# A transformer block in a written-out order: the condition's load alone on ScalarE's queue, the first loads in one row on SyncE's, and a new order of all 786 operations

## The chip, the cores and the metric

The kernel runs on one core of one Trainium2 chip. Its engines work in parallel, each through its own list of instructions: TensorE (PE; its weight loads are shown as PEld), VectorE (DVE), ScalarE (ACT), GpSimd (POOL) and SyncE (SP), which here only issues transfers. ScalarE can issue transfers too. The metric is the device time of one execution in microseconds (us).

## What is computed

One block: an attention part A and a token-mixing MLP part B, both behind a layer norm whose scale and shift come from a condition vector c. S is 2048 rows, D 512 columns, all inputs bf16.

```python
mod = silu(c) @ w_mod                      # six rows of 512: sa, ca, ga, sb, cb, gb
h = layernorm(x) * (1 + ca) + sa
x = x + ga * A(h)       # qkv = h @ wqkv; 32 heads of 16; each row attends to
                        # itself and the rows 2, 4, ..., 14 before it; then @ wo
h = layernorm(x) * (1 + cb) + sb
x = x + gb * B(h)       # layer norm, then per column: gelu(h^T @ w1 + b1) @ w2 + b2, over
                        # the 2048 rows, with 1792 hidden units
```

## The kernel before

**Operations and their order.** The kernel first describes its work as 786 named operations (`G.add`, `G.add_any`, lines 51 to 84), each with what it reads and writes, and for many with several engines to choose from. The text ORDER (lines 191 to 249) then gives the order of all of them by hand. `schedule` (86 to 125) walks through it: a letter behind a colon picks the engine (`a` ScalarE, `d` VectorE, `p` GpSimd, `s` SyncE), `q` on a TensorE operation cuts each matmul into four with 32 weight columns each, `n` leaves a matmul out whose addition another engine then makes, `+` lets VectorE make that addition. `fill:n` puts idle matmuls on TensorE, n pieces of 128 columns each (`fill_fn`, 528 to 531: in matmuls of 512 as far as they go, the rest in single pieces); they multiply the identity and are never read. `schedule` also hands out the six PSUM banks, the four `big` buffers and the five `vd` buffers in that order. Each engine executes its operations in the order of the text and waits at each one until what it needs is there; so an operation that waits holds up all that stand behind it on its engine. All instructions are issued through one helper, so they all show line 142 in the profile, and tiles tell them apart.

**The start.** SyncE and ScalarE issue the first loads: x tiles 0 and 1 (`ld_x0`, `ld_x1`, 431), the four tiles of chunk 1 in two loads (`ld_x_1_2`, `ld_x_1_4`, 455 to 458), c (`ld_c`, 429), two parts of w_mod (`ld_wmod1`, `ld_wmod0`, 434 to 437), wqkv in three parts. `dma2` (381) is a load that either queue can issue. Eight transfers can be under way without a wait; the ninth waits until the first has landed, and so on. GpSimd makes the identity; `act_table` (518) loads ScalarE's function table. `cps` (535) turns c into columns on TensorE, `silu_exp` (ScalarE) and `silu_dve` (VectorE) make silu(c). `modcols1` (551) multiplies it by a part of w_mod and gives `a1col`, the scale of the first norm, by which the weights wqkv (`wsc`, 446 to 453) or, for the first two chunks, the transposed rows (`hT`, 676 to 680) are scaled. `modcols0` gives, by a copy `sab` on ScalarE, the shift, which `qvb` (559 to 568) turns into biases of q and v. The modulation rows for all else come later (`modrow`, `mrows`, 570 to 604), over a store and a load (`st_row`, `ld_row`).

**Attention in five chunks** of 2, 4, 4, 4 and 2 tiles of 128 rows (`build_chunk`, 616 to 913). For a tile: statistics on VectorE or ScalarE (`ln1s`, with a small VectorE step `ln1v`), `rstd1` on ScalarE, `nb1` on VectorE, the normalised row (`n1`). Then the transpose (`tr` on TensorE and `hT`, or a transposing transfer `xt`), the projections on TensorE (`qkv{chunk}_{0 q, 1 k, 2 v}{part}`) and their evictions from PSUM (`ev`). Per chunk VectorE multiplies q by the shifted k (`qk`, four large products), TensorE sums over the head (`red`), VectorE takes the maximum (`max`), TensorE subtracts it (`sub`), ScalarE takes the exponent (`exp`), TensorE adds up (`esum`), ScalarE inverts (`rcp`), VectorE scales (`smB`), four transfers move the weights to other partitions (`a2`), four others copy v (`vd`); VectorE multiplies them (`pv`, four large products), TensorE sums (`pvacc`), ScalarE evicts (`oev`), and `wo` projects a tile. `x1` adds the residual, `ln2`, `n2`, `aff`, `ln3` and `h3` are the next two norms.

**The MLP.** The first matmul of B runs over the rows, so it needs the norm of all tiles. It is cut in sweeps (`mlp1_0`, `mlp1_1`, `mlp1_2`) that run as tiles get ready; between sweeps partial sums are parked in SBUF (`park`, 978) and added back (`padd`) or put in by a matmul (`inj`). `gelu` follows on ScalarE, `mlp2` for 16 row tiles on TensorE, `fin` on VectorE, `st_out` stores. The last row tile is cut in three pieces (`mlp2_15_0` to `mlp2_15_2`, 1004).

Of the kernel before, what the change touches and what calls it, by code (L numbers as in the profile page):

```python
# [197 lines left out]
qvb_cp0:a ev0_00:a ln1s12:a ev0_02:d qkv1_13 ld_wqkv2 qkv0_20 ln1v13 qk0_3 qk0_2 ev1_13:a qk0_0 qvb1 ln1v12 qkv0_22:q  # L198
ld_wrow0 red0_0 ev1_00:a qkv1_03:q ev1_10:a qk0_1 red0_1 red0_2 red0_3 mask qvb_cp1:a ev0_20:a ev0_22:a wsc1_2:p
halo_v1:a qk1_0 ev1_03:a wsc1_3:a qkv1_11:q ld_wmod2 wsc2_3:a modrow0 ld_b1 mrows0:a ev1_11:a ld_wrow2 qkv1_02 max0  # L200
wsc0_2:p ld_wo0 n1_7:p sub0 rstd1_3 qkv1_01 ld_wo2 exp0 qkv1_12:q wsc1_1:p esum0:q qk1_3 red1_0 ev1_01:a qk1_1
ev1_02:a biascols n1_6:p ld_wrow1 rcp0 smB0 ev1_12:a ld_x_4_14 ln1s14:a qkv1_22 qk1_2 a2_0_2:a xt6 ld_wrow3 modrow1
red1_1 a2_0_1:a n1_9:p wsc2_0:d ln1s15:a ln1v14 nb1_3 n1_11:a qkv1_23:q mrows1 qkv1_21 ev1_21:a red1_2 red1_3 xt8
ev1_23:a fill:1 n1_10:p qkv1_20 ev1_20:a ev1_22:a qkv2_13 qkv2_10 wsc0_1:p vd0_2 ev2_13:a ln1v15 vd0_1 max1 sub1
qkv2_00 exp1 a2_0_0:s a2_0_3:s pv0_1 vd0_0 pv0_0 st_row0 pv0_2 qkv2_03 esum1:q ld_wo3 pvacc0_0 vd0_3 halo_v2:p
biascols_cp:a pvacc0_1 pv0_3 pvacc0_2 pvacc0_3 ev2_10:a ev2_00:a qk2_0 n1_13:a n1_12:a ld_row0 woq_s rcp1 smB1
oev0_2:a qkv2_11 qkv2_02:q ev2_03:a qk2_3 qkv2_01:q red2_0 oev0_0:a wo0:q wsc2_1:a wsc2_2:a qkv2_12 ev2_11:a ev2_01:a
ev2_02:a ev2_12:a wo1 qkv2_21:q a2_1_1:a qkv2_22 x1_1:a ln2q1:a x1_0:a xt10 ln2q0:a qk2_1 qkv2_23 xt12 qk2_2 a2_1_0:s
halo_k3:a ln2m0 vd1_2 a2_1_2:s qkv3_12 a2_1_3:s pv1_2 rstd1_4 red2_1 nb1_4 vd1_0 st_row1 red2_2 red2_3 rstd2_0
ev2_22:a nb2_0 ev2_21:a qkv3_13:q ev3_13:a max2 vd1_3 pv1_0 n1_14:a vd1_1 pvacc1_2 n1_15:a qkv2_20:q ev2_20:a sub2  # L210
qkv3_22:q ev3_12:a pv1_1 qkv3_10 exp2 ev2_23:a halo_v3:a qkv3_20 n2_0:a oev1_2:a ev3_10:a esum2 rcp2 qkv3_00 ev3_22:a
qkv3_02:q ev3_00:a pv1_3 ev3_02:a pvacc1_0 ev3_20:a qkv3_01:q ev3_01:a qkv3_11:q xt14 ld_row1 n2_1:p vd2_3 pvacc1_1
smB2 aff0 qk3_0 vd2_1 fill:1 vd2_0 oev1_0:a oev1_1:a pvacc1_3 ev3_11:a qk3_1 qkv3_23:q oev1_3:a a2_2_2:s ln3s1:a
qkv3_03:q wo4 a2_2_1:s qk3_2 a2_2_0:s ev3_03:a ev3_23:a x1_4:a ln2q4:a wo2 x1_2:a a2_2_3:s red3_0 wo3:q x1_3:a ln2q3:a
qkv3_21:q ev3_21:a wo5 red3_1 pv2_3 x1_5:a vd2_2 qk3_3 qkv4_20:q red3_2 qkv4_22 red3_3 qkv4_12 fill:18 ln2q5:a
ld_w1_0_512 ln2q2:a ln2m2 pv2_0 pvacc2_0 vd3_0 ev4_20:a ln3s0:a ln3v0 ev4_12:a rstd2_2 ev4_22:a ln3v1 qkv4_02 oev2_0:a
ln2m4 rstd2_4 nb2_2 n2_2:a max3 sub3:q exp3 pvacc2_3 oev2_3:a qkv4_10:q pv2_2 vd3_2 esum3 nb2_4 pv2_1 vd3_1 n2_3:p
ld_w1_0_0 n2_5:a rcp3 smB3 pvacc2_2 fill:14 a2_3_0:s a2_3_1:s a2_3_3:s n2_4:a qkv4_00:q oev2_2:a rstd3_0 aff2 pvacc2_1
oev2_1:a wo6 wo9 wo7 aff4 nb3_0 ln3s2:d ev4_02:a ln3s3:a ln3v3 h3_1:p wo8 a2_3_2:s ev4_00:a ln3v2 ld_w2_0 ln3s4:d
rstd3_2 nb3_2 x1_9:a ln3s5:a h3_0:p mlp1_0_6_0:q x1_7:a ln3v4 x1_8:a h3_3:d mlp1_0_1_0 h3_2:d mlp1_0_6_2 mlp1_0_1_2  # L220
pv3_1 mlp1_0_5_0:q ln3v5 ev4_10:a ld_w1_0_896 x1_6:a mlp1_0_3_0:q mlp1_0_3_2:q ln2q7:a pvacc3_1 rstd3_4 mlp1_0_5_2:q
# [854 lines left out]
```

## Time and profile before

| | us |
|---|---|
| median of 3 runs | 201.75 (201.44 to 202.0) |
| the profiled execution | 202.11 |
| its span, first to last instruction | 200.4 |
| TensorE, VectorE, ScalarE, GpSimd busy | 191.0, 159.6, 128.6, 18.6 |
| matmuls, weight loads, VectorE, ScalarE instructions | 1818, 1836, 241, 306 |

The profile shows one execution. Its times count from the first instruction, so 1.7 us of the execution's time lie around the span. The rows used below have a start, a duration, the engine, the operation, out<-in tiles with shapes, the count, and in brackets the idle time of the engine ahead of it with what ended it. An engine's name with a q (ACTq, SPq) is its issuing part. A weight load shows when TensorE takes up a matmul; a matmul's own end is modelled, and matmuls overlap, so pace is read from starts.

### The profile page before, as it was taken

What the parts mean: (1) busy time and instruction counts of PE and PEld (TensorE: products, weight loads), DVE (VectorE), ACT (ScalarE), POOL (GpSimd) and SP (SyncE); (2) the same over time, 40 slices, a digit from 0 to 9 for tenths busy, and PEclk for the clock granted to TensorE, in tenths of its full rate; (3) what the DMA queues carried; (4) which work ended last, traced back from release to release, by engine and by line L of the source; (5) the groups of instructions that cost most, each with busy time, mean ns of one, the idle gap of its engine ahead of it and who ended that gap; (6) DMA issues with size and microseconds to landing.
All of it is one profiled execution on the core that took longest, in us unless ns stands there. A gap on an engine that the chain in (4) does not pass through costs nothing.

```text
span 200.4 us, 4572 instructions
## 1 busy us (share of the span) xinstructions
PE 191.0 (95%) x1818; PEld 95.8 (48%) x1836; DVE 159.6 (80%) x241; ACT 128.6 (64%) x306; POOL 18.6 (9%) x45
## 2 busy tenths in 40 slices
...
GB/s 161 341 355 350 176 240 127 160 56 185 300 143 321 220 167 194 176 112 311 64 310 257 36 184 196 160 186 234 338 244 298 85 26 52 27 52 52 174 52 52
DMA packets 53889, 35.95 MB, mean 179 GB/s; under 512 B 24428, under 2 KB 50668, under 8 KB 53868
## 3 DMA queue, kind: packets, MB, share of 16 engines
...
q10 hardware_dynamic: 1640, 0.46, 1.0%
q8 instruction: 14, 0.23, 0.5%
...
## 4 chain that ended last, share of the span: by engine, by line
PE 69%; DVE 22%; issue 4%; DMA 1%; ACT 1%; ACTq 0%; DVEq 0%
PE psS L142 67%; DVE big L142 14%; PE psL L142 3%; DVE st L142 2%; DVE h L142 2%; DMA c_t<-in_c_dram 1%; DVE mv L142 1%; ACT h L142 1%; DVE lsb L142 1%; DVE m L142 1%; DVE nb L142 0%; ACTq L142 0%; DVE woq L142 0%; DVE hT L142 0%; ACT rb L142 0%
## 5 line engine op out<-in xcount | busy, mean ns | idle before, releaser
L142 PEld LDWEIGHTS <-wst 128*128 128x128 bf16 (+1 forms) x536 | 34.9, 101 | 33.7 <-issue 4.0
L142 PE MATMUL psS<-h,wst 128*128 128x512 bf16 (+1 forms) x333 | 50.3, 380 | 0.5 <-issue 0.3
L142 DVE TENSOR_TENSOR big<-q_sb,k_f 128x4096 bf16<-128x4096 bf16 (+1 forms) x20 | 36.6, 1859 | 0.4 <-ACT q_sb L142 0.4
L142 DVE TENSOR_TENSOR big<-a2sb,vD 128x4096 bf16<-128x4096 bf16 (+1 forms) x20 | 36.5, 1860 | 0.2
L142 PE MATMUL psS<-hT,w_qkv 128*32 128x512 bf16 (+3 forms) x360 | 29.7, 346 | 0.0
L142 DVE SCALAR_TENSOR_TENSOR h<-psS,bcol,rows_bc 128x512 f32<-128x512 f32 (+2 forms) x17 | 12.1, 710 | 22.1 <-PE psS L142 20.6
L142 PEld LDWEIGHTS <-w_qkv 128*32 128x32 bf16 (+1 forms) x402 | 19.4, 109 | 17.8 <-issue 4.4
L142 PE MATMUL psS<-gT,big 128*128 128x512 bf16 x110 | 24.7, 379 | 0.1
L142 PEld LDWEIGHTS <-big 128*128 128x128 bf16 x144 | 12.0, 97 | 13.5
L142 ACT ACTIVATE junk<-xx 128x512 bf16<-128x512 bf16 x26 | 16.3, 627 | 3.3 <-DVE xx L142 1.4
L142 PE MATMUL psS<-woq,o_sb 128*32 128x512 bf16 (+1 forms) x107 | 15.7, 380 | 0.9 <-ACT o_sb L142 0.6
L142 ACT ACTIVATE gT<-psS,bcol 128x512 bf16<-128x512 f32 x14 | 9.0, 685 | 8.1 <-DVE psS L142 8.0
L142 POOL TENSOR_SCALAR h<-xx,rs,nb 128x512 bf16<-128x512 bf16 x9 | 6.9, 766 | 75.6 <-DVE nb L142 36.5
L142 DVE TENSOR_TENSOR psS<-psS,gT 128x512 f32<-128x512 f32 x14 | 9.3, 695 | 5.0 <-PE psS L142 5.0
L142 ACT ACTIVATE h<-xx,nb,rs 128x512 bf16<-128x512 bf16 x16 | 12.4, 808 | 0.5 <-DVE nb L142 0.4
L142 PEld LDWEIGHTS <-ident 128*32 128x32 bf16 (+1 forms) x137 | 7.0, 102 | 10.5 <-issue 5.9
L142 PE MATMUL psS<-ident 128*128 128x512 bf16 (+1 forms) x35 | 10.6, 450 | 1.4 <-POOL epscol L142 1.4
L142 PE MATMUL psS<-hT,wst 128*32 128x512 bf16 (+2 forms) x110 | 11.7, 352 | 0.1
L142 DVE TENSOR_TENSOR h<-h,xx 128x512 bf16<-128x512 f32 (+2 forms) x17 | 11.1, 653 | 0.6
L142 DVE TENSOR_TENSOR h<-h,rows_bc 128x1024 bf16<-128x1024 bf16 (+2 forms) x16 | 10.9, 689 | 0.4
L142 DVE BATCH_NORM_STATS2 st<-xx 128x6 f32<-128x512 bf16 x12 | 7.9, 680 | 3.9 <-DMA xx<-in_A_x_dram 3.8
L142 ACT ACTIVATE v_sb<-psS,qvb 128x512 bf16<-128x512 f32 (+1 forms) x20 | 11.0, 595 | 0.0
...
## 6 DMA issues: line engine op xcount, KB each, us to landing
...
out_dram<-h SPq DMA_DIRECT2D x15, 128.0 KB, 1.8
...
```

The source lines that it names most:

```text
L142: r = fn(*a, **k)
```

## The change

- c can be loaded by either queue (`dma2`), and the order picks ScalarE's, behind the table load. `ld_x_1_2`, which stood ahead of c on that queue, goes to SyncE, so that SyncE issues ld_x1, ld_x0, ld_x_1_4, ld_x_1_2, ld_wmod1, ld_x_2_8, ld_wqkv0 and all that follows in one row.
- The idle matmuls of the start, 4 pieces ahead of `cps`, then 64 and 4 behind it, become 6 and 68 pieces behind it. The later ones, 13, 1, 1, 18 and 14 pieces, become 13, 7, 1 and 22; 26 and 6 pieces stand behind the last store of the text.
- `tr0_0` moves ahead of `modcols1`. The four qkv0 groups of q and k now stand ahead of `modcols0`, with the 7 idle pieces between `modcols0` and `qvb0`.
- All else is in a new order. 786 names in both; some 40 operations change their engine and some 45 TensorE operations change between whole matmuls and the cut form. `wo10` makes its residual on TensorE again and `x1_10` goes from VectorE to ScalarE. `rstd1_4` and `nb1_4` move up from chunk 2 to a place ahead of `pv0`; `gsc` moves from the first output tiles to the last ones.

```diff
 ORDER = """
-ident ld_x_1_2:a halo0 ld_c consts ld_x1:s ld_x0:s ld_x_1_4:s act_table ln1s3:d fill:4 cps ld_wmod1 silu_exp silu_dve
-fill:64 ln1s1:a ln1s2:a ln1s0:d ln1v1 ld_x_2_8 ln1v0 ln1s4:d ld_wqkv0 rstd1_0 nb1_0 n1_1:a fill:4 ln1v4 n1_0:p ln1s5:d
-ln1v2 ln1v5 ln1v3 rstd1_1 nb1_1 ld_x_2_6 modcols1 n1_2:d n1_5:d ln1s8:a a1col wsc0_3:p n1_4:d tr0_0 hT0_1:a hT0_3:a
-n1_3:d hT0_0:a fill:13 hT0_2:a ld_wqkv1 ld_wmod0 ln1s9:d ld_x_3_10 ln1s6:d tr1_0 tr1_2 hT1_2:a ln1v6 qkv0_02 ln1v9
-hT1_0:a qkv0_12 qkv0_10 ln1s7:d ln1v7 ln1v8 rstd1_2 hT1_3:d wsc1_0:a ev0_12:a modcols0 sab:a ld_x_3_12 nb1_2 n1_8:a
-qkv0_00 qvb0 wsc0_0:p ev0_10:a ld_b2 ld_wo1 hT1_1:d qkv1_00 ln1s11:d ln1s10:d ln1s13:d qkv1_10:q ln1v11 ln1v10
...
+ident act_table ld_c:a cps silu_exp silu_dve ld_x1:s ln1s1:d ln1v1 ld_x0:s ln1s0:a ld_x_1_4:s ld_x_1_2:s ln1v0
+ld_wmod1 ln1s3:d rstd1_0 ln1s5:d nb1_0 ln1v3 n1_0:p ln1s4:d ln1v5 ln1s2:a ln1v2 halo0 fill:6 n1_1:p fill:68 tr0_0
+ld_x_2_8 ln1v4 ld_wqkv0 consts rstd1_1 nb1_1 n1_5:a n1_2:d n1_3:d ln1s9:d modcols1 a1col ld_x_2_6 n1_4:a ln1s8:d
+wsc0_1:p ln1v8 hT0_3:a tr1_2 hT0_1:a ld_wqkv1 ld_wmod0 ld_x_3_10 wsc1_3:p hT0_2:a wsc0_2:d hT0_0:a tr1_0 ln1s6:d
+fill:13 hT1_1:a qkv0_02:q ld_x_3_12 qkv0_00 ld_wo3 hT1_0:d hT1_3:a qkv0_12 hT1_2:a wsc1_2:a ln1v9 ln1s7:d wsc0_0:p
+ln1v6 ln1v7 rstd1_2 ev0_12:a nb1_2 n1_6:a qkv0_10 ln1s10:d modcols0 sab:a wsc1_1:p ld_wqkv2 n1_7:a ln1s11:d fill:7
+qvb0 qvb_cp0:a ln1s13:d ev0_10:a ev0_00:a qkv1_03 qkv1_10 ln1s12:a ev1_10:a ln1v10 qkv1_00 ln1v13 ev0_02:d ev1_03:a
...
+a2_0_0:s rstd1_4 a2_0_3:s red1_2 red1_3 max1 qkv2_00:q n1_11:a qkv1_20 ev2_00:a nb1_4 st_row0 ev1_20:a
...
+fin10_0 st_out10_0 st_out8_0 fin11_0 st_out11_0 fin13_0 st_out13_0 mlp2_12_0 mlp2_14_0 fin12_0 mlp2_15_0 gsc fin14_0
+st_out12_0 st_out14_0 fin15_0 st_out15_0 mlp2_15_1 fin15_1 mlp2_15_2 st_out15_1 fin15_2 st_out15_2 fill:26 fill:6
 """
...
-    add("act", 0.55, lambda: nc.scalar.dma_start(c_t[:], c[0].rearrange("(t p) -> t p", p=P)), writes=["c_t"],
-        name="ld_c", lat=2.0)
+    dma2(c_t[:], c[0].rearrange("(t p) -> t p", p=P), D * 4, ["c_t"], "ld_c")
```

More of the change, by code (lines that the diff above doesn't have):

```diff
@@ L197 @@
-qkv0_00 qvb0 wsc0_0:p ev0_10:a ld_b2 ld_wo1 hT1_1:d qkv1_00 ln1s11:d ln1s10:d ln1s13:d qkv1_10:q ln1v11 ln1v10
[L198 to L221, printed above, removed]
@@ L227 @@
-mlp1_0_7_0 ld_w2_3 park0_4:a ln3v6 mlp1_0_7_2 park0_5:a ln3v9 x1_11:a ln2q12:a mlp1_0_8_0 mlp1_0_8_2 park0_6:a wo13:n
-ln3s7:a ln3v7 sub4 mlp1_0_10_0 mlp1_0_9_0 x1_13:d exp4 rstd3_6 nb3_6 esum4 mlp1_0_8_4 ln2q13:a ln2m12 mlp1_0_10_2
-mlp1_0_10_4 mlp1_0_9_2 rcp4 mlp1_0_7_4 h3_8:d rstd2_12 mlp1_0_12_0 mlp1_0_12_2 mlp1_0_12_4 smB4 a2_4_1:a a2_4_0:s
-mlp1_0_9_4 a2_4_2:s h3_9:d a2_4_3:a h3_7:d nb2_12 h3_6:p mlp1_0_7_6 ln2q11:a park0_7:a x1_10:d mlp1_0_8_6 ld_w1_0_1664
-ln2q10:a park0_8:a n2_13:p mlp1_0_9_6 park0_9:a n2_12:d aff12 ln2m10 rstd2_10 mlp1_0_10_6 park0_10:a ln3s13:a pv4_2
@@ new lines @@
+qkv1_13 qk0_1 red0_1 red0_2 red0_3 wsc0_3:p ev0_20:a qk1_0 ld_wo1 ld_wrow2 mask ev1_13:a qkv1_01:q n1_8:a ld_wo0 max0
+wsc2_3:a ld_wrow3 ld_wrow0 ln1s14:a qkv1_11:q ev1_11:a modrow1 xt6 qk1_3 ev1_01:a ld_wmod2 sub0:q exp0 qkv1_22
+ev1_22:a qkv1_02 qk1_1 esum0:q vd0_3 xt8 ln1v12 ev1_02:a vd0_0 rcp0 smB0 qkv1_12:q vd0_1 ev1_12:a qk1_2 wsc2_2:d
+rstd1_3 a2_0_1:a nb1_3 mrows1 modrow0 a2_0_2:a mrows0:a ln1v14 red1_0 red1_1 qkv1_23 halo_v1:p ln1s15:a ln1v15 qkv1_21
+ev1_21:a a2_0_0:s rstd1_4 a2_0_3:s red1_2 red1_3 max1 qkv2_00:q n1_11:a qkv1_20 ev2_00:a nb1_4 st_row0 ev1_20:a
```

65 lines of the change are left out of this document (43 added, 22 removed).

## The prediction

> **What bounds the kernel now.** I read the page first, then the windows by stage, then the chain of waits in order of time. On the page the line of busy times, and the shares of the chain by engine:
>
> ```profile
> PE 191.0 (95%) x1818; PEld 95.8 (48%) x1836; DVE 159.6 (80%) x241; ACT 128.6 (64%) x306; POOL 18.6 (9%) x45
> ...
> PE 69%; DVE 22%; issue 4%; DMA 1%; ACT 1%; ACTq 0%; DVEq 0%
> ```
>
> TensorE looks like the one bound, but the averages hide stages. Busy time by stage (stretch, its length, then PE, PEld, DVE, ACT, POOL, each with its count):
>
> ```profile
> 19.00:42.00 23.00, 22.72 (x388) 12.80 (x383) 22.60 (x23) 20.52 (x47) 2.00 (x3) 1.00 0.71 171
> 42.00:58.00 16.00, 15.43 (x184) 6.73 (x184) 15.76 (x14) 14.47 (x32) 0.77 (x1) 1.00 0.58 180
> 58.00:104.00 46.00, 44.77 (x625) 22.80 (x628) 45.63 (x50) 44.59 (x112) 2.46 (x4) 1.00 0.69 209
> 104.00:121.00 17.00, 16.76 (x113) 7.95 (x118) 16.55 (x35) 14.83 (x41) 1.53 (x2) 1.00 0.66 177
> ...
> 132.00:198.00 66.00, 65.01 (x325) 30.96 (x329) 36.84 (x56) 10.25 (x15) 0.00 (x0) 1.00 0.49 141
> ```
>
> From 19 to 121 us VectorE is idle for 0.40 + 0.24 + 0.37 + 0.45 = 1.46 us of 102: it is full, and ScalarE nearly so. A TensorE row counts as busy while its pipeline drains, so its 0.3 to 1.2 us of idle time hide the small stalls in which it follows VectorE. From 132 us on VectorE has room and TensorE alone is full. Three places of the chain, and the hand-over from VectorE to TensorE in the timeline:
>
> ```profile
> 1.33 2.60 DMA c_t<-in_c_dram
> ...
> 104.91 3.40 PE psS L142 x15
> ...
> 197.36 0.29 DVE h L142
> ```
> ```profile
> 117.03 3.49 DVE L142 TENSOR_TENSOR big<-a2sb,vD 128x2048 bf16<-128x2048 bf16 x3
> ...
> 121.98 1.89 PE L142 MATMUL psS<-woq,o_sb 128*128 128x512 bf16 x8
> ```
>
> The first thing on the chain is the load of the condition c. The last attention product ends on VectorE at 117.03 + 3.49 = 120.52; wo14 starts behind it (reduction, eviction) at 121.98, and from there TensorE runs to 197.3. So the end is a sum: **start of VectorE's full stretch (first product qk0, 18.80), plus VectorE's work up to pv4, plus VectorE's waits in it, plus TensorE's fixed rest.** A shorter TensorE stream before 120 us buys nothing unless VectorE gets there earlier, too.
>
> **The change, part by part.**
>
> *Same work.* The names of both orders are the same 786. On TensorE one matmul of 512 columns comes (wo10 takes its residual on TensorE again). The idle pieces between the first normalisation and the last product go from 51 to 43 pieces of 128 columns, and runs in the 32-column form are entered 22 times and not 23. All of that lies in the stretch where TensorE follows VectorE, whose full list hides it: nothing, either way (without that cover wo10's matmul costs 0.22 and the pieces save 0.4). 32 idle pieces go behind the last real matmul.
>
> *c.* Rows of the start: the issue on ScalarE's queue ahead of c, the table load, the row of idle matmuls, and two weight loads that show its pace.
>
> ```profile
> 0.82 0.48 ACTq L142 DMA_DIRECT2D xx<-in_A_x_dram  x1
> ...
> 1.98 1.28 ACT L142 ACT_TABLE_LOAD   x1 [1.98 <-issue]
> ...
> 4.10 6.58 PE L142 MATMUL psS<-ident 128*128 128x512 bf16 x17
> ...
> 9.19 0.15 PEld L142 LDWEIGHTS <-ident 128*128 128x128 bf16 x1 [0.28 <-issue]
> ...
> 9.62 0.57 PEld L142 LDWEIGHTS <-ident 128*128 128x128 bf16 x3 [0.28 <-issue]
> ```
>
> Before, c is issued at 1.33, behind 256 KB of x, and landed at 3.93. Afterwards only the table load stands ahead of it. Whether that holds the issue, no row of the start shows; later rows show an issue beside the instruction ahead of it, and how fast a short transfer can land:
>
> ```profile
> 46.73 0.60 ACT L142 ACTIVATE k_f<-psS 128x512 bf16<-128x512 f32 x1
> 46.79 0.62 ACTq L142 DMA_DIRECT2D a2sb<-lsb  x1
> ```
> ```profile
> out_dram<-h SPq DMA_DIRECT2D x15, 128.0 KB, 1.8
> ```
>
> Ends: 0.85 + 1.8 = 2.65; 0.85 + 2.60 = 3.45; and, if the load holds it, 0.82 + 1.28 + 2.60 = 4.70. I take 2.85 (issue beside the table load, a little over the 1.8): **-1.1 us** against 3.93.
>
> *Idle matmuls of 6 and 68 pieces.* Behind c stood 17 matmuls of 512 columns; now 18 of them and two of 128. One takes 9.62 - 9.19 = 0.43 us until 9.62 and then 0.22 (the last four, 9.62 to 10.52, the row of modcols1 below). With the same time until the pace doubles, the additional 1.5 matmuls cost **+0.3**. Their end, F, was 10.52 and becomes 10.52 - 1.1 + 0.3 = 9.7.
>
> *The order from F to the first product.* Rows of before: modcols1, tr0, the first hT evictions, three qkv0 groups, modcols0, the fourth, qvb0, then VectorE's q eviction and qk0.
>
> ```profile
> 10.52 0.54 PE L142 MATMUL psS<-sc,big 128*128 128x1 bf16 x16
> 10.92 0.61 PE L142 MATMUL psS<-ident,h 128*128 128x128 bf16 x8
> ...
> 13.19 2.78 PE L142 MATMUL psS<-hT,wst 128*128 128x256 bf16 x24
> 15.81 0.54 PE L142 MATMUL psS<-sc,big 128*128 128x1 bf16 x16
> 16.21 1.05 PE L142 MATMUL psS<-hT,wst 128*128 128x256 bf16 x8
> 17.09 0.67 PE L142 MATMUL psS<-sab,wst 128*128 128x1 bf16 x16
> ```
> ```profile
> 18.00 0.69 DVE L142 TENSOR_TENSOR q_sb<-psS,qvb 128x512 bf16<-128x512 f32 x1 [0.25 <-ACT qvb L142]
> ...
> 18.80 1.23 DVE L142 TENSOR_TENSOR big<-q_sb,k_f 128x2048 bf16<-128x2048 bf16 x1
> ```
>
> Before, the fourth qkv0 group (16.21 to 17.09) covered ScalarE's copy of sab, which qvb0 needs. Now modcols0 stands behind all four groups, sab's copy is covered by 7 idle pieces alone (896 columns, 0.38 us at 0.22 for 512). modcols1 stands behind tr0, so that a1col, which all hT evictions need, comes at F + 1.2 and not F + 0.6; the evictions, which waited for tr0 until F + 1.0, start 0.2 later. From F to qvb0 that is one group, +0.87, less the part of it that covered more than the 0.38 does (0.87 + 0.01 gap - 0.38 = about -0.5), +0.2 for a1col, +0.2 for a normalisation that now stands ahead of sab on ScalarE, and +0.2 for one group in the 32-column form between full ones: **+1.0**, with ends of +0.6 (the last two at nothing) and +1.2. qvb0, the copy, the eviction and qk0 follow at the old distance: 18.80 - 1.1 + 0.3 + 1.0 = **19.0, +0.2**. VectorE has a little less to do ahead of this point; as it waits there for qvb, that is idle time and no gain.
>
> *SyncE's queue.* x_1_2 leaves ScalarE's queue for fourth place on SyncE's, so w_mod is issued one issue later (0.48). The stretch in which it lands:
>
> ```profile
> 4.00:11.00 7.00, 7.00 (x36) 2.93 (x37) 4.54 (x17) 5.99 (x18) 0.77 (x1) 1.00 1.00 320
> ```
>
> 1,280 KB up to and with w_mod take 4.0 us at 320 GB/s: some 7 to 8 us, ahead of F at 9.7. Without that cover F could not come forward, and the -1.1 and +0.3 would be lost (+0.8). Later, three of the four a2_4 transfers stand in one row on SyncE in place of two: one issue (0.62) later, beside the normalisations ahead of pv4; without them +0.6. The loads of the modulation rows and of the later weights change places on this queue; I cost that at nothing, hidden by the products that VectorE does ahead of their first use.
>
> *VectorE's list from qk0 to pv4.* Three operations of one tile come (n2_10, n2_13, h3_6), h3_7 and x1_10 go, one statistics step of 0.2 (as at 34.94 below) slips behind qk0:
>
> ```profile
> L142 DVE TENSOR_SCALAR h<-h,rs,nb 128x512 bf16<-128x512 bf16 x5 | 1.9, 409 | 0.0
> ```
> ```profile
> 112.64 0.68 DVE L142 SCALAR_TENSOR_TENSOR xx<-psS,xx 128x512 bf16<-128x512 f32 x1
> 113.25 0.08 DVE L142 DVE_READ_ACCUMULATOR xx<-psS,xx 128x1 f32 x1
> ```
>
> 0.2 + 3 x 0.41 - 0.41 - 0.76 (0.68 and the read of its sum, 0.08) = **+0.2**. The other moves between engines are swaps of like for like.
>
> *A new wait.* ln1v15, a small VectorE step, stands ahead of max1 and all four pv0; it waits for ScalarE's ln1s15. Behind it now stands nb1_4 too, which moved up from 54 us and waits for rstd1_4.
>
> ```profile
> 17.16 0.59 ACT L142 ACTIVATE k_f<-psS 128x512 bf16<-128x512 f32 x1
> ...
> 20.67 0.60 ACT L142 ACTIVATE k_f<-psS 128x512 bf16<-128x512 f32 x1 [0.46 <-PE psS L142]
> ```
> ```profile
> 28.21 1.27 ACT L142 ACTIVATE q_sb<-psS,qvb 128x512 bf16<-128x512 f32 x2 [0.27 <-PE psS L142]
> ...
> 34.53 0.19 ACT L142 ACTIVATION_READ_ACCUMULATOR junk<-xx 128x1 f32 x1
> ```
> ```profile
> 34.94 0.23 DVE L142 SCALAR_TENSOR_TENSOR mv<-mv,st 128x1 f32<-128x1 f32 x1
> ```
>
> ev0_10 (0.59) now follows qvb's copy, which itself is some 0.4 late: ScalarE is 1.0 behind. Its old waits of 0.46 and 0.27 swallow 0.7. ln1s15 then ends at 34.72 + 0.3 to 1.0, while VectorE arrives at 34.94 + 0.2: between 0 and 0.6 of wait. I take **+0.2**.
>
> *Behind the end.* The last real matmuls end at 197.3; 32 idle pieces at the quick pace (about 1.8 us) end near 199.1, beside the landing of the last store, which ends the span of 200.4. Nothing; if they were held until that landing, up to 1.8.
>
> **Sum** against the profiled execution (202.11 us, span 200.4, 1.7 around it): +0.2 + 0.2 + 0.2 = +0.6, so 202.7. That execution is 0.36 above the median of 201.75; the same +0.6 on the median gives 202.35. I forecast **202.4**.
>
> **The rivals.**
>
> *Faster: the idle row ends early.* c lands at 2.65 (-0.2), the pace doubles 1 us sooner after the row's start (about 2.3 matmuls at 0.22 in place of 0.43: -0.5), ScalarE is then in time and the 0.2 of wait goes, too. Then 202.4 - 0.9 = 201.5; with +0.6 for the order (-0.4): 201.1. For: all these sit on one chain. Against: VectorE's list is no shorter, so qk0's start is all there is to win. It decides once qk0 starts before 18.3. That the pace doubles at different times has a rule beside it: the Trainium skill (TensorE: Matmul & The Clock Gate, Part 1) has the clock doubled at the end of a busy window of about 3.4 us that runs free of the kernel. By it the row would take 3.4 to 6.8 us to speed up; the 5.5 us here (4.10 to 9.62) fits, and by an estimate from that page F could move by some 0.9 us either way.
>
> *Slower: the table load holds c.* c at 4.70 in place of 2.85: +1.85, so 204.2. For: in before the load starts 0.04 behind the end of c's issue, in order. Against: the pair at 46.73. The Trainium skill (ScalarE: Activation LUTs, What ACT_TABLE_LOAD costs) adds a drain of about 1.4 us to a load that switches sets; no row here shows it, and by an estimate from that page the time would be 205.6.
>
> *Slower: many small waits.* Before, VectorE waits almost never. In a wholly new order ScalarE's late start may show at smB0, qk1 and nb1_4 as well, and again before pv4: four places at the 0.37 that one such place cost (below) are +1.5, so 203.9.
>
> ```profile
> 28.93 2.29 DVE L142 TENSOR_TENSOR big<-q_sb,k_f 128x4096 bf16<-128x4096 bf16 x1 [0.37 <-ACT q_sb L142]
> ```
>
> *The queue does nothing for c.* The transfers share the DMA engines, which have 768 KB of x to move at that time: c at 3.45, +0.6, so 203.0.
>
> **How the numbers follow.** Forecast 0.35, early row 0.22, table load 0.10, many waits 0.21, shared engines 0.12. The forecast's own spread (201.8 to 203.0) lies on both sides of 202.35, a little more of it below. A measurement of this kernel can tell about 0.3% (0.6 us) from no change: below 201.15 faster, above 202.35 slower. The early row gives most of faster, 0.19; same is 0.20 of the forecast and the rest of the early row, 0.23; slower is the rest of the forecast and the three slower rivals, 0.58. Range: 200.9 (the early row with 0.2 to spare) to 204.2 (the table load).
>
> **What would show it.** c's matmul near 2.9; the idle row ending near 9.7; qk0 near 19.0; VectorE busy over 99% from there; a wait of VectorE at 35 us with ScalarE's name; wo14 near 122.6; the span ending 78.4 us behind wo14 as before. Wrong would be: a c matmul after 3.5; VectorE idle for over 2 us between qk0 and pv4; a gap on TensorE behind 132 us; or the last idle pieces behind the last store.

## The result and the profile after

| | before | after |
|---|---|---|
| median, lowest to highest (11 executions each) | 201.51 (201.25 to 202.12) | 203.39 (202.53 to 204.02) |
| the profiled execution, its span | 202.11, 200.4 | 202.82, 200.8 |
| time outside the span | 1.7 | 2.0 |

The change costs 1.9 us from median to median; the ratio over all executions is 1.0084, with a 95% interval of 1.0066 to 1.0101. Forecast was 202.4, with a range of 200.9 to 204.2. The direction was right and the range held; the sum (+0.6) was a third of what came.

The two profiles side by side show only +0.7, because of which executions they are: that of before lies 0.6 above its median, that of after 0.6 below. Whoever reads only this pair looks for the wrong amount. So the experiments below also serve as further profiles of the same two orders. First the lines of after that answer to those of before. The page, busy times and shares of the chain (of after the profile follows the chain back for 72% of the span only, so the shares can't be compared one by one):

```profile
PE 194.1 (97%) x1798; PEld 97.7 (49%) x1798; DVE 160.2 (80%) x241; ACT 128.2 (64%) x305; POOL 19.6 (10%) x43
...
PE 51%; DVE 10%; ACT 9%; issue 2%; DVEq 0%
```

Windows by stage (stretch, length, PE, PEld, DVE, ACT, POOL):

```profile
19.00:42.00 23.00, 22.17 (x353) 12.31 (x351) 22.23 (x24) 20.41 (x45) 3.23 (x3) 1.00 0.72 175
42.00:58.00 16.00, 15.85 (x109) 6.87 (x107) 15.72 (x14) 13.67 (x32) 0.77 (x1) 1.00 0.66 205
58.00:104.00 46.00, 44.29 (x579) 22.57 (x581) 45.53 (x49) 44.22 (x112) 4.68 (x5) 1.00 0.73 213
104.00:121.00 17.00, 17.00 (x158) 8.05 (x154) 16.36 (x35) 15.56 (x45) 0.00 (x0) 1.00 0.46 116
```

VectorE is idle for 0.77 us from 19 to 42 (0.40 before), TensorE for 0.83 (0.28 before); from 42 to 104 little differs. The new idle time lies in the first chunks. The timeline of the start:

```profile
0.81 1.28 ACT L142 ACT_TABLE_LOAD   x1 [0.81 <-PEq L1059]
0.85 0.57 ACTq L142 DMA_DIRECT2D c_t<-in_c_dram  x1
...
2.26 0.18 PE L142 MATMUL psS<-ident,c_t 4*128 4x4 bf16 x1 [2.26 <-DMA c_t<-in_c_dram]
...
8.83 0.61 PE L142 MATMUL psS<-ident,h 128*128 128x128 bf16 x8
9.28 0.54 PE L142 MATMUL psS<-sc,big 128*128 128x1 bf16 x16
...
17.89 1.23 DVE L142 TENSOR_TENSOR big<-q_sb,k_f 128x2048 bf16<-128x2048 bf16 x1
...
121.96 1.26 PE L142 MATMUL psS<-woq,o_sb 128*32 128x512 bf16 x20
```

c's issue runs beside the table load, c is there at 2.26, the idle row ends at 8.83, and the first product starts at 17.89, 0.91 earlier than before. Yet wo14 starts at 121.96, where it was (121.98). Between the two places 0.9 us are lost. VectorE's scaling step smB0 (the first row) and its first product pv0 in the kernel before, where neither waits:

```profile
31.14 0.42 DVE L142 TENSOR_TENSOR lsb<-lsb,rb 128x512 bf16<-128x512 bf16 x1
...
36.22 2.35 DVE L142 TENSOR_TENSOR big<-a2sb,vD 128x2048 bf16<-128x2048 bf16 x2
```

Rows of TensorE and of VectorE from the timeline of after, 26 to 41 us:

```profile
26.19 0.85 PE L142 MATMUL psS<-gT,sc 128*32 128x128 bf16 x48 [0.38 <-DMA gT<-in_w_mod_dram]
26.87 0.39 PE L142 MATMUL psL<-m,nident 128*32 128x512 bf16 x4
```
```profile
30.27 0.43 DVE L142 TENSOR_TENSOR lsb<-lsb,rb 128x512 bf16<-128x512 bf16 x1 [0.40 <-ACT rb L142]
...
31.01 2.29 DVE L142 TENSOR_TENSOR big<-q_sb,k_f 128x4096 bf16<-128x4096 bf16 x1 [0.32 <-ACT k_f L142]
...
34.35 0.92 DVE L142 SCALAR_TENSOR_TENSOR mv<-mv,st 128x1 f32<-128x1 f32 x2
35.19 1.21 DVE L142 TENSOR_REDUCE m<-psL 128x128 bf16<-128x1024 f32 x1
36.33 0.14 DVE L142 SCALAR_TENSOR_TENSOR nb<-mv,rs 128x2 f32<-128x2 f32 x1
36.39 4.62 DVE L142 TENSOR_TENSOR big<-a2sb,vD 128x2048 bf16<-128x2048 bf16 x4
```

The 48 small matmuls are modrow1. It reads all four loads of modulation rows (gT), and TensorE stands idle ahead of it until the last one lands. Behind it, in TensorE's order, stands sub0, the second step of chunk 0's softmax: sub0, exp0, esum0, rcp0, and VectorE waits at smB0 (0.40). The wait's bracket names ScalarE (rb), but ScalarE had itself waited for TensorE, and TensorE for a transfer. In the order of the kernel before, modrow1 stands behind smB0. TensorE's waits from 18 to 40 us (for what, us in total, times, longest) of after and of before, where no transfer is among them:

```profile
PE psS L142 <- DMA gT<-in_w_mod_dram: 0.4, 1, 0.4
```
```profile
PE psS L142 <- issue: 0.2, 1, 0.2
```

The second place is at 34.35: two small statistics steps (ln1v14, ln1v15) took 0.92 us together; the last section shows them at 0.34.

The same places in eight profiles, with the distance from the first product to pv0 (us; the first five rows are the changed order with sub0 behind modrow1, then two with one of the two kernels' orders altered at this place, then before):

| kernel | qk0 | modrow1 | sub0 | smB0 | pv0 | end of pv4 | wo14 | qk0 to pv0 |
|---|---|---|---|---|---|---|---|---|
| after | 17.89 | 26.19 | 26.87 | 30.27 | 36.39 | 120.82 | 121.96 | 18.50 |
| after, ln1v15 behind max1 | 17.92 | 26.52 | 27.20 | 30.60 | 36.96 | 121.67 | 122.80 | 19.04 |
| after, no idle pieces at the end | 18.30 | 26.96 | 27.64 | 31.05 | 37.19 | 121.82 | 122.95 | 18.89 |
| after, six GpSimd instructions more | 18.49 | 27.60 | 28.28 | 31.68 | 37.70 | 122.16 | 123.29 | 19.21 |
| after, idle row four longer | 18.56 | 26.54 | 27.22 | 30.62 | 36.16 | 120.56 | 121.71 | 17.60 |
| after, modrow1 behind esum0 | 18.67 | 28.96 | 26.41 | 30.56 | 37.12 | 121.55 | 122.68 | 18.45 |
| before, modrow1 ahead of sub0 | 18.15 | 26.15 | 26.93 | 31.15 | 36.23 | 120.51 | 121.96 | 18.08 |
| before | 18.80 | 30.90 | 26.93 | 31.14 | 36.22 | 120.52 | 121.98 | 17.42 |

In the first five rows smB0 follows modrow1 by 4.08 or 4.09 us each time, whatever qk0 does (17.89 to 18.56). In the first four of them TensorE waits for the load of the modulation rows (0.38 to 1.39 us): its landing has taken the place of the first product as the start of the chain, and it differs by 1.4 us between these profiles, which fits the wider spread of the executions (1.5 us and not 0.9). In the fifth TensorE doesn't wait for it. From pv0 to wo14 the orders are equal: 85.76 before, 85.55 to 85.84 in the first six rows. So what the change loses on the path is lost ahead of pv0. The last column shows it without any comparison of early and late executions: in before and in the four runs below that keep its order behind the start it is 17.27 to 17.43, wherever qk0 lies (18.29 to 20.06); in the first five rows it is 17.60 to 19.21.

### The profile page after: what moved, and what is told of

The parts are those of the page before. It is cut to its first block, busy times and chain, and to the rows that moved or that the text cites. A ratio compares the mean times of both kernels' runs of the same rounds, so it can differ in the third digit from the quotient of the medians.

```text
span 200.8 us, 4507 instructions
## 1 busy us (share of the span) xinstructions
PE 194.1 (97%) x1798; PEld 97.7 (49%) x1798; DVE 160.2 (80%) x241; ACT 128.2 (64%) x305; POOL 19.6 (10%) x43
## 4 chain that ended last, share of the span: by engine, by line
PE 51%; DVE 10%; ACT 9%; issue 2%; DVEq 0%
PE psS L142 51%; DVE big L142 6%; ACT junk L142 2%; ACT v_sb L142 2%; DVE h L142 1%; ACT h L142 1%; ACT o_sb L142 1%; ACT xx L142 1%; DVE lsb L142 1%; ACT q_sb L142 1%; DVE m L142 1%; ACT k_f L142 1%; DVE mv L142 1%; PE psL L142 1%; ACT lsb L142 1%
## 5 line engine op out<-in xcount | busy, mean ns | idle before, releaser
L142 PEld LDWEIGHTS <-wst 128*128 128x128 bf16 (+1 forms) x560 | 35.4, 101 | 33.8 <-issue 3.9
L142 PE MATMUL psS<-h,wst 128*128 128x512 bf16 (+1 forms) x350 | 51.0, 379 | 0.5 <-ACT h L142 0.4
L142 DVE SCALAR_TENSOR_TENSOR h<-psS,bcol,rows_bc 128x512 f32<-128x512 f32 (+2 forms) x17 | 12.1, 710 | 23.2 <-PE psS L142 22.8
L142 PEld LDWEIGHTS <-big 128*128 128x128 bf16 x144 | 12.0, 97 | 13.2
L142 PE MATMUL psS<-woq,o_sb 128*32 128x512 bf16 (+1 forms) x148 | 16.6, 380 | 0.4 <-ACT o_sb L142 0.4
L142 ACT ACTIVATE junk<-xx 128x512 bf16<-128x512 bf16 x24 | 15.1, 627 | 1.2 <-DMA xx<-in_A_x_dram 0.8
L142 POOL TENSOR_SCALAR h<-xx,rs,nb 128x512 bf16<-128x512 bf16 x8 | 6.1, 770 | 86.9 <-DVE nb L142 50.8
L142 ACT ACTIVATE h<-xx,nb,rs 128x512 bf16<-128x512 bf16 x17 | 13.4, 814 | 1.6 <-DVE nb L142 1.6
L142 PEld LDWEIGHTS <-ident 128*128 128x128 bf16 (+1 forms) x132 | 7.9, 103 | 9.2 <-issue 5.4
L142 PE MATMUL psS<-hT,wst 128*32 128x512 bf16 (+3 forms) x124 | 11.6, 333 | 0.0
L142 PEld LDWEIGHTS <-group 128*32 128x32 bf16 x288 | 7.0, 95 | 9.5 <-issue 4.1
L142 PE MATMUL psS<-ident 128*128 128x512 bf16 (+1 forms) x47 | 11.5, 400 | 0.0
```

What stands on the lines that cost most here:

```text
L142: r = fn(*a, **k)
```

## The experiments

Ratios are against the kernel before, timed with each group on the same chip (medians 201.38 to 201.59).

### The order around modrow1

**modrow1 behind esum0** (after)

```diff
-ev1_11:a modrow1 xt6 qk1_3 ... qk1_1 esum0:q vd0_3 xt8
+ev1_11:a xt6 qk1_3 ... qk1_1 esum0:q modrow1 vd0_3 xt8
```

> The changed kernel with one operation moved: modrow1, 48 small matmuls that need all four loads of modulation rows, from ahead of sub0 to behind esum0. In the changed kernel TensorE stands idle ahead of it until the last of these loads lands (0.38 us in the profiled run, 0.68 and 1.39 in two other profiles of the same start), with sub0, exp0, esum0, rcp0 and smB0 behind it, and VectorE's wait at smB0 was 0.40, 0.70 and 1.23 in the same profiles; the landing (26.1 to 27.6) differs from run to run. Theory A, this is the step that failed, and the source of the runs' spread: the idle time ahead of sub0 goes, VectorE's wait at smB0 goes, and the end comes 0.4 to 1.3 earlier: 202.3, lowest to highest under 1.2 us (1.5). Theory B, the wait at smB0 only moves to the first pv0 product, whose transfers are as late as before: 203.2.

Measured: 203.07 (202.32 to 203.51), ratio 1.0070 (1.0047 to 1.0094). VectorE of this kernel, 30 to 38 us:

```profile
30.56 0.42 DVE L142 TENSOR_TENSOR lsb<-lsb,rb 128x512 bf16<-128x512 bf16 x1
31.36 2.29 DVE L142 TENSOR_TENSOR big<-q_sb,k_f 128x4096 bf16<-128x4096 bf16 x1 [0.38 <-ACT k_f L142]
...
34.70 0.92 DVE L142 SCALAR_TENSOR_TENSOR mv<-mv,st 128x1 f32<-128x1 f32 x2
...
37.12 2.36 DVE L142 TENSOR_TENSOR big<-a2sb,vD 128x2048 bf16<-128x2048 bf16 x2 [0.30 <-DMA a2sb<-lsb]
```

The idle time ahead of sub0 and at smB0 is gone: smB0 comes 11.9 us behind qk0; in the first five rows of the table it was 12.1 to 13.2. The runs lie within 1.2 us. But the median fell by 0.3 only, as theory B had it, and the interval overlaps that of after (1.0066 to 1.0101), so that the gain isn't clear of the noise. Two waits further on take most of it, the held statistics steps (0.92) and the transfers of the weights (a2sb).

**modrow1 ahead of sub0, in the kernel before**

```diff
-qkv1_11:q ld_wmod2 wsc2_3:a modrow0 ld_b1 mrows0:a ... ld_wo0 n1_7:p sub0 ... n1_6:p ld_wrow1 rcp0 ... xt6 ld_wrow3 modrow1
+qkv1_11:q ld_wrow3 wsc2_3:a ld_b1 ... ld_wo0 ld_wrow1 n1_7:p modrow1 sub0 ... n1_6:p rcp0 ... xt6 ld_wmod2 modrow0 mrows0:a
```

> The kernel before with the suspected step of the change put in alone: modrow1 stands ahead of sub0 with all four loads of modulation rows ahead of that of w_mod's third part, and modrow0 with its copy mrows0 takes modrow1's old place. Start and all else as before, so the first product starts as before and sub0 could run at 26.0 to 26.9. Theory A, TensorE waits there for the last of the four loads as in the changed kernel (landing 25.5 to 27.6 by the profiles so far) and then takes 0.68 us for modrow1: sub0 at 26.9 to 28.3, VectorE idle ahead of smB0 for 0.4 to 1.2, the end 0.5 to 1.2 later than before: 202.3. Theory B, the order behind sub0 is what costs and not this step: 201.5, no idle time ahead of smB0.

Measured: 202.23 (201.81 to 202.81), ratio 1.0039 (1.0022 to 1.0056): 0.6 to 0.8 later, from this step and the loads and modrow0 that trade places with it. TensorE and VectorE of this kernel:

```profile
26.15 0.85 PE L142 MATMUL psS<-gT,sc 128*32 128x128 bf16 x48
26.93 0.39 PE L142 MATMUL psL<-m,nident 128*128 128x512 bf16 x1
```
```profile
28.94 2.29 DVE L142 TENSOR_TENSOR big<-q_sb,k_f 128x4096 bf16<-128x4096 bf16 x1 [1.03 <-ACT q_sb L142]
```

Theory A's time is right, its mechanism only half. The loads were there, and TensorE didn't wait. But modrow1 itself puts sub0 at 26.93, with qk0 at 18.15; in the kernel before sub0 is at 26.93 with qk0 at 18.80. The 0.65 us that this execution had gained at the start are used up by 0.78 us of matmuls in front of sub0, and VectorE's idle time (1.03) shows ahead of a product of chunk 1. So here the place costs about 0.65 even without a late load (18.08 from qk0 to pv0, 17.42 in before). What of it is modrow1 and what the later place of modrow0 and its copy, no run separates.

**A longer idle row** (after)

```diff
-fill:6 n1_1:p fill:68 tr0_0
+fill:6 n1_1:p fill:84 tr0_0
```

> The changed kernel with 84 idle pieces in the place of 68 (four matmuls of 512 columns, 0.86 us at the quick pace). Theory A, the load of the modulation rows decides when sub0 can run, so an earlier or later first product is worth little: qk0 0.8 later at 18.7 to 19.3, TensorE's wait ahead of modrow1 shorter by as much, the end 0 to 0.3 later: 203.4 to 203.7. Theory B, the start is a chain that goes through to the end: 204.2.

Measured: 202.96 (202.44 to 203.70), ratio 1.0069 (1.0045 to 1.0093). Four matmuls more at the start cost nothing; the median is even 0.4 below that of after, inside the spread. That speaks for theory A: this part of the start has slack. In the profile TensorE doesn't wait for the load at all and the small waits behind it are gone too, and qk0 to pv0 takes 17.60: without these waits the new order is nearly as fast there as the old one.

### The next waits

**ln1v15 behind max1** (after)

```diff
-ln1s15:a ln1v15 qkv1_21 ev1_21:a a2_0_0:s rstd1_4 a2_0_3:s red1_2 red1_3 max1 qkv2_00:q
+ln1s15:a qkv1_21 ev1_21:a a2_0_0:s a2_0_3:s red1_2 red1_3 max1 ln1v15 rstd1_4 qkv2_00:q
```

> The changed kernel with ln1v15 and rstd1_4 moved from ahead of max1 to behind it. In the changed kernel ln1v15 took 0.70 us and not 0.22 and ended together with a GpSimd normalisation. Theory A, VectorE is held there by GpSimd and the path runs through it: max1 starts at 34.6 and not 35.2, ln1v15 takes 0.22, pv0 starts 0.4 to 0.6 earlier, and 0.4 arrives at the end: 203.0. Theory B, the next wait of VectorE takes the gain (ScalarE and TensorE are full there as well): pv0 earlier, the last product as before, 203.4.

Measured: 203.68 (203.39 to 203.81), ratio 1.0104 (1.0086 to 1.0122). VectorE of this kernel:

```profile
34.81 1.22 DVE L142 TENSOR_REDUCE m<-psL 128x128 bf16<-128x1024 f32 x1
35.94 0.21 DVE L142 SCALAR_TENSOR_TENSOR mv<-mv,st 128x1 f32<-128x1 f32 x1
36.75 0.16 DVE L142 SCALAR_TENSOR_TENSOR nb<-mv,rs 128x2 f32<-128x2 f32 x1 [0.60 <-ACT rs L142]
36.96 2.36 DVE L142 TENSOR_TENSOR big<-a2sb,vD 128x2048 bf16<-128x2048 bf16 x2
```

The hold is gone (0.21), max1 runs 0.4 earlier although smB0 was 0.3 later than in after, and nb1_4, which stands ahead of pv0, gives all of it back: its rstd1_4 now comes later (0.60). Theory B by the time and by its reason, the next wait; only pv0 came not earlier but later (36.96 and 36.39).

**The three edits together** (after; those of the two runs above and of the run with six more GpSimd instructions below)

> The changed kernel with three edits together: modrow1 behind esum0, ln1v15 and rstd1_4 behind max1, six more GpSimd instructions. Theory A, three places of one sum: the first run of this list, less 0.3 for the clearing at the end, less up to 0.4 for the hold of VectorE at 35 us, as that gain now isn't taken back by late transfers: 201.6. Theory B, the hold at 35 us is taken back by the next wait as when it was moved alone: 202.0.

Measured: 202.74 (202.54 to 203.01), ratio 1.0058 (1.0039 to 1.0076). 0.65 below after, a smaller gain than either theory's, and half of it is the clearing at the end (0.33, below). The executions lie within 0.5 us (1.5 in after), and no modulation row is waited for ahead of sub0 any more; but those of the run with ln1v15 behind max1, where it is waited for, lie within 0.4, so that the spread proves nothing here. nb1_4 still waits 0.60, made by the move of ln1v15.

**nb1_4 behind the second pv0 product as well** (after; the diff is against the three edits together)

```diff
-esum0:q modrow1 vd0_3 ... qkv1_12:q vd0_1
+esum0:q vd0_3 ... qkv1_12:q modrow1 vd0_1
...
-ev2_00:a nb1_4 st_row0 ... pv0_1 pv0_0
+ev2_00:a st_row0 ... pv0_1 nb1_4 pv0_0
```

> The run with three edits (202.74) with two more: nb1_4 from ahead of the first pv0 product to behind the second, since VectorE waited 0.60 us there for ScalarE, and modrow1 behind qkv1_12, since VectorE waited 0.37 us for that group's eviction. Theory A, both waits are on the path: 0.6 + 0.1 earlier, 202.0. Theory B, the a2_0 transfers, which land 3.4 to 4.9 us behind their issue in the changed order (2.1 in the kernel before), are next: pv0 starts at most 0.3 earlier, 202.5.

Measured: 202.43 (202.20 to 203.81), ratio 1.0061 (1.0035 to 1.0087). VectorE of this kernel:

```profile
34.59 1.23 DVE L142 TENSOR_REDUCE m<-psL 128x128 bf16<-128x1024 f32 x1 [0.45 <-PE psL L142]
...
36.48 2.36 DVE L142 TENSOR_TENSOR big<-a2sb,vD 128x2048 bf16<-128x2048 bf16 x2 [0.55 <-DMA a2sb<-lsb]
```

Theory B: both waits went, max1 now waits for TensorE (0.45) and pv0 for the a2_0 transfers (0.55). The ratio is that of the three edits (1.0058), so these two moves gained nothing that can be told. Four waits stood one behind the other in front of pv0 (the load, the hold, nb1_4, the transfers), and each that was taken away showed the next. No version of the changed order came down to the kernel before.

### The end

**No idle pieces behind the end** (after)

```diff
-fin15_2 st_out15_2 fill:26 fill:6
+fin15_2 st_out15_2
```

> The changed kernel without the 32 idle pieces behind the last real matmul. Theory A, as predicted, they lie beside the landing of the last store and cost nothing: 203.4, the last store's issue and its landing as in the changed kernel. Theory B, they hold the closing of the program in most runs, though not in the profiled one, where they end 0.2 us ahead of the landing: 202.5, and less spread between the runs.

Measured: 203.25 (202.28 to 203.69), ratio 1.0074 (1.0050 to 1.0098). Theory A: they cost nothing that can be measured.

**Six GpSimd instructions more** (after)

```diff
+    more = sb.tile([P, 6], F32, name="more")
...
         o.fn()
+        if o.name == "h3_13":
+            for j in range(6):
+                nc.gpsimd.memset(more[:, j:j + 1], 0.0)
```

> The changed kernel with six more GpSimd instructions behind its last normalisation (six stores of zero into columns that nobody reads); no other instruction is touched. In the changed kernel GpSimd's last clearing instruction starts 0.36 us behind the one ahead of it (0.03 in the kernel before), and the time of all its runs stands 2.0 us above the span (1.7 in the kernel before); GpSimd has four instructions fewer than before. Theory A, GpSimd's list ends on another side of a block of instructions that has to be fetched: with six more the clearing starts at once, and the time outside the span falls back to 1.7, so 203.39 - 0.33 - 0.3 = 202.8. Theory B, the late clearing and the longer time outside have nothing to do with the length of GpSimd's list: 203.4.

Measured: 202.90 (201.70 to 203.67), ratio 1.0060 (1.0034 to 1.0086). The closing instructions of before, after and this kernel (start of the first and of the last of each kind); the last rows of the three fences are GpSimd's clearing:

```profile
L1071 SPq DRAIN  x3: 7/7/13, 199.6 to 199.9; - x3
...
L1071 POOLq EVENT_SEMAPHORE_RANGE_CLEAR  x1: 96/96/96, 200.0 to 200.0; - x1
```
```profile
L1070 SPq DRAIN  x3: 7/7/13, 199.7 to 200.0; - x3
...
L1070 POOLq EVENT_SEMAPHORE_RANGE_CLEAR  x1: 96/96/96, 200.4 to 200.4; - x1
```
```profile
L1074 SPq DRAIN  x3: 7/7/13, 201.0 to 201.4; - x3
...
L1074 POOLq EVENT_SEMAPHORE_RANGE_CLEAR  x1: 96/96/96, 201.4 to 201.4; - x1
```

After SyncE's last step the clearing follows within 0.1 us in before and here, after 0.4 in the changed kernel. The other profiles agree: in all five of the changed order with its own GpSimd list it is 0.4, in all three with six instructions more and in all six made from the kernel before it is 0.1 or less. So half of theory A holds: 0.33 us of the change come from the length of GpSimd's list (the times alone, 202.90 and 203.39, have too wide a spread to show it). The other half fell: the time outside the span stayed at 2.0 in most of the executions (1.70 to 2.06). Why the clearing is late stays open. The profiles count transfers of instructions from 199 to 204 us, two in after, one here and none in before; but in after they come at 201.1 and 202.5, behind the clearing at 200.4, so it can't have waited for them.

### The start alone

**c alone on ScalarE's queue** (before)

```diff
-ident ld_x_1_2:a halo0 ld_c consts ld_x1:s ld_x0:s ld_x_1_4:s act_table ln1s3:d fill:4 cps ld_wmod1 silu_exp silu_dve
-fill:64 ln1s1:a ln1s2:a ln1s0:d ln1v1 ... ln1s4:d ... n1_1:a fill:4 ln1v4
+ident act_table ld_c:a halo0 consts ld_x1:s ld_x0:s ld_x_1_4:s ld_x_1_2:s cps ld_wmod1 silu_exp silu_dve
+fill:68 ln1s1:a ln1s0:d ln1v1 ... ln1s3:d ln1s4:d ... n1_1:a fill:4 ln1s2:a ln1v4
```

> The kernel before with the start of the change alone: c on ScalarE's queue behind the table load, x_1_2 fourth on SyncE's, no idle pieces ahead of c's matmul and 68 + 4 behind it; two statistics steps move behind the tile's later landing; everything from the first transpose on in the old order. Theory A, the start is a chain: c lands at 2.2 (3.93), the end of the idle row comes at 9.0 to 9.3 (10.52), qk0 about 1.2 earlier at 17.6, and the end 0.8 to 1.2 earlier: 200.5. Theory B, the weights bind (they land at 10.36 and 12.47 in the kernel before, and one issue later here): the idle row ends earlier, qk0 stays at 18.6 to 18.9, 201.5. Theory C, VectorE's later waits swallow it as they did in the changed kernel: qk0 at 17.6, the last product as before, 201.5.

Measured: 202.29 (201.86 to 204.92), ratio 1.0055 (1.0026 to 1.0083). The start of TensorE in the profiled execution, which is the shortest of the 12:

```profile
5.77 2.32 PE L142 MATMUL psS<-ident 128*128 128x512 bf16 x10
8.75 0.55 PE L142 MATMUL psS<-sc,big 128*128 128x1 bf16 x16 [0.66 <-DMA big<-in_w_mod_dram]
9.16 0.61 PE L142 MATMUL psS<-ident,h 128*128 128x128 bf16 x8
9.61 0.87 PE L142 MATMUL psS<-ident 128*128 128x512 bf16 x4
10.57 0.23 PE L142 MATMUL psS<-ident,h 128*128 128x128 bf16 x1
11.61 1.01 PE L142 MATMUL psS<-ident,h 128*128 128x128 bf16 x15 [0.81 <-DVE h L142]
```

None of the three theories. The row ends near 8.0 (5.77 and ten matmuls of 0.22), and then w_mod (8.7) and a normalised tile (11.6) are late: qk0 comes at 18.29, inside the 18.15 to 19.14 of the three profiles with the old start. Four of the 12 executions were 1.5 to 3 us longer. Of the 0.8 between the medians about 0.35 lie outside the span (2.04 to 2.16 here, 1.7 in before).

**c first, x_1_2 second on ScalarE's queue** (before; the diff is against the run above)

```diff
-ident act_table ld_c:a halo0 consts ld_x1:s ld_x0:s ld_x_1_4:s ld_x_1_2:s cps
+ident act_table ld_c:a ld_x_1_2:a halo0 consts ld_x1:s ld_x0:s ld_x_1_4:s cps
```

> The kernel before with c first and x_1_2 second on ScalarE's queue, behind the table load (the run with c alone had x_1_2 fourth on SyncE's queue); all else as in that run: 68 + 4 idle pieces behind c's matmul, nothing ahead of it. The run with c alone had 201.9 to 202.7 in eight executions and 203.8 to 204.9 in four. Theory A, the long executions come from the first loads in one row on SyncE's queue (w_mod and the weights each one issue later): without it no execution above 203, median 201.0 to 201.5. Theory B, they come from the idle row that starts at 2.4: it ends before the work behind it is there, or before the pace has doubled, whichever way the loads are queued: the same two groups.

Measured: 203.25 (201.94 to 203.93), ratio 1.0071 (1.0042 to 1.0099): six executions from 201.9 to 202.8 and six from 203.7 to 203.9, so theory B. This time the profile caught a long one (203.70). Windows (the figure behind POOL is the granted clock) and TensorE:

```profile
8.00:12.00 4.00, 2.12 (x33) 1.31 (x31) 2.50 (x10) 3.46 (x12) 1.05 (x2) 1.00 1.09 373
12.00:15.00 3.00, 3.00 (x26) 2.36 (x27) 2.72 (x10) 2.59 (x7) 1.77 (x3) 0.64 1.11 341
15.00:18.00 3.00, 3.00 (x36) 2.57 (x34) 2.34 (x7) 1.38 (x4) 2.88 (x4) 0.79 1.08 345
18.00:21.00 3.00, 2.92 (x41) 1.76 (x41) 1.72 (x3) 2.89 (x8) 0.06 (x1) 1.00 0.92 333
```
```profile
10.51 0.23 PE L142 MATMUL psS<-ident,h 128*128 128x128 bf16 x1 [0.69 <-DVE h L142]
11.93 1.01 PE L142 MATMUL psS<-ident,h 128*128 128x128 bf16 x15 [1.19 <-DVE h L142]
12.78 4.45 PE L142 MATMUL psS<-hT,wst 128*128 128x256 bf16 x24
```

TensorE had 1.9 us of idle time from 9.8 to 11.9; from 12.8 on 24 matmuls took 4.45 us (2.78 in before, at 13.19). The clock falls back for 3.4 us: the granted clock is 0.50 from 12.84 to 16.25 and 1.00 on both sides (the two windows agree: 0.36 x 3 + 0.21 x 3 = 1.7). And qk0 is late by as much as these executions are longer: 20.06, 1.8 behind the run above.

**The gap filled** (before; the diff is against the run with c alone)

```diff
-n1_3:d hT0_0:a fill:13 hT0_2:a
+n1_3:d hT0_0:a fill:37 hT0_2:a
```

> The run with c alone on the kernel before (median 202.29, eight executions of 12 below 202.7, four at 203.8 to 204.9), with 37 idle pieces in the place of 13 ahead of tr1: six more matmuls of 512 columns where TensorE stood idle. In the long execution that was profiled (c first, x_1_2 second) the granted clock was 0.64 from 12 to 15 us and 0.79 from 15 to 18, behind 1.9 us in which TensorE was idle. Theory A, the idle time behind a row that ends early takes the pace away in some executions: with it filled no execution is above 203, median 202.0 to 202.4. Theory B, the pace falls for another reason: two groups as before.

Measured: 202.46 (202.19 to 202.87), ratio 1.0054 (1.0036 to 1.0073). Theory A: no long execution. There are six only; with four of 12 long, as in the run with c alone, six short ones in a row come by chance about once in eleven times, so the cause is likely and not proven. The profile with c alone also had idle time there, 1.5 us, and kept a clock of 1.00. The Trainium skill (TensorE: Matmul & The Clock Gate, Part 1) has windows of 3413 ns that run free, and the clock halved after an idle one. The length of the drop agrees (3.41 us); but in the long execution 1.9 us idle in the 3.4 us ahead of it were enough, the stretch need not be empty.

**The table load first** (before)

```diff
-ident ld_x_1_2:a halo0 ld_c consts ... ld_x_1_4:s act_table ln1s3:d
+ident act_table ld_x_1_2:a halo0 ld_c consts ... ld_x_1_4:s ln1s3:d
```

> The kernel before with the table load as ScalarE's first instruction, ahead of the issues of x_1_2 and c; nothing else is moved. The time of a run stands 1.68 to 1.79 us above its span where the start is the old one (11 executions) and 2.0 to 2.16 in the two kernels before with c alone and in most executions of the changed kernel, where the table load comes first and c is the first issue on ScalarE's queue. Theory A, the table load's place makes this time: 2.0 or more here, the span as before, 201.8. Theory B, something else in the new start makes it (the queue on which c or the x tiles go, the idle pieces): 1.7 here, the span as before, 201.5.

Measured: 201.62 (201.01 to 202.47), ratio 0.9999 (0.9986 to 1.0012); outside the span 1.68 to 1.79. The table load's place costs nothing, neither on the path nor outside. What in the new start makes the 0.3 us outside the span stays open; the queue of x_1_2 doesn't, as the run with x_1_2 on ScalarE's queue has 2.06 to 2.15. As this kernel is the one before in all but one issue, its 12 spans (199.3 to 200.7, median 199.9) also tell that the span of before's profile, 200.4, is a late one.

## Why the prediction was right in sign and wrong in size

The sum as it was measured, from median to median (+1.9): outside the span +0.3; GpSimd's clearing +0.33; TensorE from wo14 to the last result +0.1 (75.67 before, 75.80 after); and ahead of pv0 about +1.25. This last one is an estimate and not in any single pair of profiles: the median span of after is 0.6 above its profile (pv0 36.39, so about 37.0), that of before 0.5 below (36.22, so about 35.7). The four make 2.0; spans are told to 0.1 only. Of the 1.25, modrow1's place gave 0.65 when it was put into the kernel before; the rest lies in the waits behind it, and no run shows it apart.

That the sign was right is in part luck. Of the three terms that made +0.6, qk0's later start (+0.2) didn't come, VectorE's list (+0.2) grew by nothing beside the hold, and the wait at ln1v15 (+0.2) came as something else; what made the change slower had been costed at nothing or stood in no term.

- **c.** Forecast -1.1, by an issue beside the table load: -1.7 (2.26 against 3.98 for its matmul). The rival in which the table load holds c was wrong, and so was the one in which the shared engines hold it.
- **Idle row and order up to qk0.** Row's end forecast for 9.7, it was 8.83, and 8.04 to 9.22 in the profiles of the same row; from there to qk0 9.06 us against 8.28, +0.8, forecast +1.0. qk0 was forecast 0.2 later; it came 0.9 earlier in this pair of profiles. But that of before is a late one: with 17.4 from qk0 to pv0, a pv0 at 35.7 puts qk0 near 18.3 by an estimate, and the seven profiles with the changed start have it at 17.89 to 18.67, with 18.30 in the middle. So the earlier c gained about nothing at qk0. The row's end moves with the time until the pace doubles, 3.4 to 6.0 us after c's matmul in all 14 profiles. The free-running window of the Trainium skill (TensorE: Matmul & The Clock Gate, Part 1), which gives 3.4 to 6.8 by an estimate, agrees.
- **The bound.** "Start of VectorE's full stretch, plus its work, plus its waits, plus TensorE's fixed rest" held before and told the rival with the early row to win once qk0 starts before 18.3. It did in after's profile, at 17.89, and won nothing: in the new order another chain starts the stretch.
- **The step that failed** is one sentence under SyncE's queue: "The loads of the modulation rows and of the later weights change places on this queue; I cost that at nothing, hidden by the products that VectorE does ahead of their first use." The first use isn't behind VectorE's products. It is modrow1 on TensorE, moved from behind smB0 to ahead of sub0, with a load that lands at 26.1 to 27.6 in front of it. The move of modrow1 into the kernel before shows the cost: 0.6 to 0.8 in time, and 18.08 from qk0 to pv0 in place of 17.42. The move out of the changed kernel shows the waits at sub0 and smB0 gone, but no gain clear of the noise, as other waits follow. That a waiting operation holds up all that stand behind it on its engine was applied to ln1v15 and not to modrow1.
- **Many small waits** (203.9, chance 0.21) was the rival that came closest. Of its four places smB0, the chunk 1 products and nb1_4 showed up; the cause it gave, ScalarE's late start, was not the first one.
- **VectorE's list.** Forecast +0.2 (its own terms add up to 0.26). Busy time from qk0 to the end of pv4: 100.26 before, 100.77 after, of which 0.5 is the hold; without it, nothing.
- **The wait at ln1v15.** Forecast +0.2 with ScalarE's name. In the profile ScalarE was just in time (34.54, the step starts at 34.57); the 0.5 us were a hold by GpSimd (below). In the run without the idle pieces it was ScalarE (0.52). Moving it gained nothing, as nb1_4 followed.
- **VectorE busy over 99% from qk0** was wrong: 2.16 us idle of 102.93, 1.46 of 101.72 before. Over 2 us idle was one of the signs of being wrong that the prediction had named.
- **Idle pieces behind the end, w_mod ahead of F, a2_4 on SyncE**: nothing, as forecast; but with c alone in the old order, where the row ends earlier, TensorE waited 0.66 for w_mod. GpSimd's clearing and the time outside the span were in no term.
